# Two more attention pairs take the block-transposed load: pairs 6 and 7 of 32, one core

## The chip, the cores and the metric

The kernel runs on one core of a Trainium2 chip. The metric is device time in microseconds (us), the median over the runs shown. A core has a matrix engine (TensorE, PE in the profile; its weight loads are listed apart as PEld), VectorE (DVE), ScalarE (ACT), GpSimd (POOL) and SyncE (SP), which here issues nearly all DMAs. Each engine works through its own list of instructions in a fixed order and waits on semaphores for the others.

## The reference

The inputs are q, k and v of shape (8 batches, 8 heads, 576 tokens, 64), a feature matrix w_phi (64, 128), and float64 matrices of a token mixer (U, V) and of a channel MLP (w_ch1, w_ch2). Linear attention comes first, per batch and head:

```
def phi(x):
    proj = np.einsum('bhsd,df->bhsf', x, w_phi)
    proj = proj - np.max(np.abs(proj), axis=-1, keepdims=True)
    return np.concatenate([np.exp(proj), np.exp(-proj)], axis=-1)
q_p, k_p = (phi(q), phi(k))
kv = np.einsum('bhsf,bhsd->bhfd', k_p, v)
z = np.sum(k_p, axis=2)
num = np.einsum('bhsf,bhfd->bhsd', q_p, kv)
den = np.einsum('bhsf,bhf->bhs', q_p, z)[..., None] + 1e-06
return (num / den).astype(np.float32)
```

Then, with x of shape (8, 576, 512), u = x + (x^T U V)^T, and the output is u + relu(u w_ch1) w_ch2.

## The kernel before

**Pairs.** Attention is done for two heads of a batch at a time, a pair: four pairs in each of eight batches, 32 pairs, numbered here 0 to 31 as 4b + j. The 576 tokens of a head are 512 main tokens and a tail of 64. A `Pair` loads k and q (`raw`, two buffers, one for k and one for q), turns them so that the head dimension lies on the partitions (`transposes`), multiplies with w_phi (`project_k`, `project_q`), takes the maximum and the two exponentials (`k_features`, `q_features`), sums k features times v over the tokens (`kv_main`), and multiplies q features with the result (`out_main`).

**Two ways through a pair.** The flag `self.split` (L253) chooses. Without it (batches 0 and 1, pairs 0 to 7), k and q come in one DMA each of 256 KB (L270); TensorE turns them with eight 128x128 transposes (L322), ScalarE copies each result out of PSUM (L327), and the projections are plain float32 matmuls against the zero-padded `w_two` (L383 for k, L426 for q). A float32 matmul shows as two records in the trace. With it (batches 2 to 7, pairs 8 to 31), k and q come in eight DMAs of 32 KB each (L264), so that each 32x32 block lands where a transposition inside the blocks leaves the operand turned. VectorE turns the blocks in place (L314), ScalarE writes a rounded high part of each half (L317), VectorE the remainder (L318), and the projections are single-pass matmuls on these parts: L398 for k, whose two part sums are put together by a ScalarE copy (L401) and a VectorE addition (L402); L421 and L422 for q. The tail of 64 tokens is turned by TensorE in both ways (L304) and is split into parts by `stack` (L295, L296) only in the second. The order in which v is loaded (L286) and in which `out_main` writes follows the same flag.

**Buffers that order the pairs.** There is one `raw` buffer for k and one for q (L258). The loads of a pair start when the pair before has let go of them: in the first way after TensorE's transposes, in the second after the VectorE remainders at L318. `T0` and `T1`, the turned operands, have one buffer each; `T1` of a pair is free once the pair before it has made its second q projection.

**The weights and the MLP.** The float64 weights come in as words by DMA (L209, L212), sixteen blocks of two matrices. They are issued in the step of a pair behind that pair's last raw load (`issue_after(far.loaded.ins)`, with `LOADS`), and are converted block by block by ScalarE (L137, L138, L140, L234), VectorE (L141, L234, L235) and GpSimd (L145), spread over the steps 24 to 63 and ahead of their first use. The MLP of a batch (`hidden` L618, `add` L639, with `h_hi` L623 and `h_lo` L624) is cut into 32 chunks, which are mixed into the attention steps of later pairs. The MLP of batch 0 starts when batch 0 has its tokens mixed, some 92 us into the run, and runs beside pairs 5 to 9.

**What sets the order.** In the loop over pairs, step n projects k and q of pair n+1, makes the output of pair n, and loads and turns pair n+2 (`far`). The program is then ordered once, before it runs, by a scheduler that simulates the engines; on the chip each engine keeps to that order.

Of the kernel before, what the change touches and what calls it, by code (L numbers as in the profile page):

```python
# [25 lines left out]
def tile_kernel(  # L26
# [24 lines left out]
    NPAIR = H // 2  # L51
# [192 lines left out]


    SPLIT, Q = 2, 32

    class Pair:


        def __init__(self, b, j):
            self.b, self.h0, self.nm = b, 2 * j, f"{b}_{j}"
            self.split = b >= SPLIT  # L253
            self.tail = slice((b % 2) * ST, (b % 2 + 1) * ST)
            nm, hs = self.nm, slice(self.h0, self.h0 + 2)
            self.raw = []
            for n, src in enumerate((k, q)):
                m = raw.tile([P, 2, SM // 2], F32, tag="raw", bufs=2, name=f"raw{nm}_{n}")  # L258
                if self.split:
                    for i in range(4):  # L260
                        rs = slice(i // 2 * (SM // 2), (i // 2 + 1) * (SM // 2))
                        cs = slice(i % 2 * Q, (i % 2 + 1) * Q)
                        for g in range(2):
                            self.loaded = nc.sync.dma_start(  # L264
                                out=m[i * Q:(i + 1) * Q, g, :].rearrange(
                                    "c (j r) -> c j r", r=Q),
                                in_=src[b, self.h0 + g, rs, cs].rearrange(
                                    "(j c) r -> c j r", c=Q))
                else:
                    self.loaded = nc.sync.dma_start(  # L270
                        out=m, in_=src[b, hs, 0:SM, :].rearrange("h (p t) d -> p h (t d)", t=NT))
                self.raw.append(m)

            self.t_r = raw.tile([P, 2 * D], F32, tag="t_r", bufs=1, name=f"t_r{nm}")
            for n, src in enumerate((k, q)):
                nc.sync.dma_start(
                    out=self.t_r[n * ST:(n + 1) * ST, :].rearrange("r (h d) -> r h d", h=2),
                    in_=src[b, hs, SM:S, :].rearrange("h r d -> r h d"))
# [653 lines left out]
```

## The time and the profile before

| | |
|---|---|
| median of 3 runs | 1218.15 us (1218.03 to 1224.73) |
| the profiled execution | 1218.74 us, span 1216.9 us from first to last instruction |
| mean granted TensorE clock | 0.997 |
| busy: DVE, ACT, POOL | 668.7, 538.9, 204.5 us |
| DMA | 100.61 MB, mean 83 GB/s |

The span is the time from the first to the last instruction on the core; the profiled execution's own time is 1.84 us longer. The busy time of PE is that of matmul records, whose ends are modelled and which overlap, so that the mean duration of a record is longer than the time by which it holds back the next. The chain of work that ended last gives that second time, piece by piece. What belongs to one pair is told by the order of the records: of line 322 there are eight in each of pairs 0 to 7. The last two groups of eight, at 106.5 and 148.6 us, are those of pairs 6 and 7; line 314, which stands for pairs 8 to 31, starts at 157.1 us.

### The profile page before, as it was taken

The page shows a single profiled execution, that of the slowest core. Times are in us where ns is not written, and L with a number is a line of the kernel's source. Part 1 is how long each engine was busy: PE and PEld are TensorE (multiplying, and loading weights), DVE is VectorE, ACT ScalarE, POOL GpSimd, SP SyncE. Part 2 cuts the span into 40 slices and gives each one's busy share as a digit, 9 for nine tenths or more (in the row PEclk, how much of TensorE's full clock was granted, in tenths as well). Part 3 has the DMA queues.
Part 4 walks back from the last instruction along what each step waited for, and adds up shares of the span by engine and source line. Part 5 has one row for each costly group of instructions (what it writes and reads, how often), then busy time and mean ns, then how long its engine had stood idle before and what let it go on. Part 6 is the DMA issues. An engine that isn't in the chain of part 4 may idle for free.

```text
span 1216.9 us, 18254 instructions
## 1 busy us (share of the span) xinstructions
PE 1195.1 (98%) x6669; PEld 1031.3 (85%) x6669; DVE 668.7 (55%) x1482; ACT 538.9 (44%) x1151; POOL 204.5 (17%) x154
## 2 busy tenths in 40 slices
PE   8999998999999999999999999999999999999998
PEld 7878887888888888888888888888888888888886
DVE  5866777765556556755556656665656542311211
ACT  6867787454534445354435444344444431111110
POOL 3543443111111112011111111011101110000000
PEclk9999999999999999999999999999999999999999
DMA  4886021421245123431354123521343015410201
GB/s 132 262 279 210 29 50 28 134 64 30 65 108 116 30 52 79 109 81 25 72 125 104 28 59 88 120 46 33 99 92 99 1 53 149 115 35 1 69 1 35
DMA packets 248410, 100.61 MB, mean 83 GB/s; under 512 B 215424, under 2 KB 227968, under 8 KB 248320
## 3 DMA queue, kind: packets, MB, share of 16 engines
q1 hardware_dynamic: 248000, 98.92, 31.4%
q8 instruction: 53, 0.87, 0.3%
q10 hardware_dynamic: 320, 0.52, 0.1%
q14 instruction: 37, 0.30, 0.1%
HBM read 78.41 MB, written 20.97 MB: 82 GB/s over the span
## 4 chain that ended last, share of the span: by engine, by line
PE 80%; DVE 7%; SPq 5%; DMA 3%; ACT 3%; issue 2%; POOL 0%; DVEq 0%; ACTq 0%; POOLq 0%
PE ph L618 28%; PE o L639 28%; PE xp L481 7%; PE kv_ps L442 7%; SPq L604 3%; PE pp L560 2%; PE pk L398 1%; SPq L264 1%; PE kv_ps L435 1%; PE pq L421 1%; DMA u_dram<-x 1%; DMA y<-u_dram 1%; PE xpt L468 1%; PE pq L422 1%; DVE T L318 1%
## 5 line engine op out<-in xcount | busy, mean ns | idle before, releaser
L618 PE MATMUL ph<-uT_hi,w 128*128 128x512 f32 x1152 | 389.4, 395 | 1.2 <-ACT uT_hi L242 1.2
L639 PE MATMUL o<-w,h_hi 128*128 128x512 f32 x1152 | 329.4, 397 | 3.2 <-ACT h_hi L623 3.2
L618 PEld LDWEIGHTS ph<-uT_hi,w 128*128 128x128 f32 x1152 | 216.4, 188 | 46.9 <-ACT uT_hi L242 1.8
L639 PEld LDWEIGHTS o<-w,h_hi 128*128 128x128 f32 x1152 | 212.0, 189 | 45.6 <-ACT h_hi L623 4.9
L618 PE MATMUL ph<-uT_lo,w 128*128 128x512 f32 x576 | 225.1, 391 | 0.2 <-DVE uT_lo L243 0.2
L623 ACT ACTIVATE h_hi<-ph 128x512 fp32r<-128x512 f32 x144 | 86.0, 597 | 271.4 <-PE ph L618 260.4
L624 DVE SCALAR_TENSOR_TENSOR h_lo<-ph,h_hi 128x512 fp32r<-128x512 f32 x144 | 98.7, 686 | 176.9 <-ACT h_hi L623 175.7
L639 PE MATMUL o<-w,h_lo 128*128 128x512 f32 x576 | 192.1, 395 | 0.0
L362 POOL PARTITION_ALL_REDUCE qp<-qp x64 | 126.8, 1981 | 289.2 <-ACT qp L361 270.7
L481 PEld LDWEIGHTS xp<-kv,qp 128*128 128x128 f32 x1024 | 122.9, 192 | 4.8 <-ACT qp L365 1.3
L618 PEld LDWEIGHTS ph<-uT_lo,w 128*128 128x128 f32 x576 | 108.3, 188 | 21.5 <-DVE uT_lo L243 0.7
L442 PEld LDWEIGHTS kv_ps<-vb,kp 128*128 128x128 f32 x1024 | 124.0, 192 | 2.8
L442 PE MATMUL kv_ps<-vb,kp 128*128 128x65 f32 x1024 | 123.5, 270 | 0.0
L481 PE MATMUL xp<-kv,qp 128*128 128x65 f32 x1024 | 122.9, 272 | 0.6 <-ACT qp L365 0.6
L639 PEld LDWEIGHTS o<-w,h_lo 128*128 128x128 f32 x576 | 105.4, 188 | 20.2
L352 ACT ACTIVATE kp<-kp 128x512 f32<-128x512 f32 x64 | 40.4, 632 | 132.1 <-DVE kp L349 82.8
L362 POOL PARTITION_ALL_REDUCE qp_t<-qp_t x32 | 27.1, 846 | 399.8 <-ACT qp_t L361 399.8
L318 DVE TENSOR_TENSOR T<-raw,T 64x512 fp32r<-64x512 f32 x96 | 69.2, 720 | 33.4 <-ACT T L317 30.9
L314 DVE STREAM_TRANSPOSE raw<-raw 128x512 f32<-128x512 f32 x48 | 34.1, 711 | 83.3 <-DMA raw<-in_q_dram 34.3
L317 ACT CAST T<-raw 64x512 fp32r<-64x512 f32 x96 | 59.3, 618 | 33.5 <-PE pq L422 20.6
L364 ACT ACTIVATE qp<-qp 128x512 f32<-128x512 f32 x64 | 40.4, 632 | 55.4 <-DVE qp L363 54.8
L145 POOL INT64_ADD w_ab<-w_ab x32 | 44.7, 1398 | 69.3 <-DVE w_ab L141 68.5
(125 smaller groups left out, 1324.5 us busy)
## 6 DMA issues: line engine op xcount, KB each, us to landing
words<-in_moe_w_ch_dram SPq DMA_DIRECT2D x32, 512.0 KB, 9.0
w<-kept SPq DMA_DIRECT2D x30, 512.0 KB, 4.0
vb<-in_v_dram SPq DMA_DIRECT2D x64, 128.0 KB, 2.4
u_dram<-x SPq DMA_DIRECT2D x32, 256.0 KB, 2.2
st<-u_dram SPq DMA_DIRECT2D x16, 512.0 KB, 3.8
out_dram<-st SPq DMA_DIRECT2D x32, 256.0 KB, 2.4
y<-u_dram SPq DMA_DIRECT2D x112, 64.0 KB, 2.4
raw<-in_k_dram SPq DMA_DIRECT2D x192, 32.0 KB, 2.0
```

What stands on the lines that cost most here:

```text
L145: nc.gpsimd.int64_add(a64, a64, b64)
L317: nc.scalar.copy(out=m[here, s, :], in_=x_[here])
L318: nc.vector.tensor_sub(m[there, s, :], x_[here], f32(m[here, s, :]))
L352: nc.scalar.activation(out=kp[:, :, 0:F], in_=kp[:, :, F:2 * F], func=AF.Exp)
L362: nc.gpsimd.partition_all_reduce(qp[:, 0, :], qp[:, 1, :], P, ReduceOp.absmax)
L364: nc.scalar.activation(out=qp[:, 0, :], in_=qp[:, 1, :], func=AF.Exp)
L442: nc.tensor.matmul(self.kv_v[:, f, g, :], kp[:, t, f * F:(f + 1) * F], self.vb[:, g, t, :], start=False, stop=(t == NT - 1), skip_group_ch ...
L481: nc.tensor.matmul(xv[:, c, :], qp[:, f, c * P:(c + 1) * P], self.kv[:, f, c // 2 if self.split else s, :], start=(f == 0), stop=(f == 1))
L618: nc.tensor.matmul(ph, w1_part(f, l, c), r[:, c, :], start=(n == 0), stop=(n == 3 * NCC - 1))
L623: on_act = nc.scalar.activation(out=h_hi, in_=ph, func=AF.Relu)
L624: on_dve = nc.vector.scalar_tensor_tensor(out=h_lo, in0=ph, scalar=0.0, in1=f32(h_hi), op0=ALU.max, op1=ALU.subtract)
L639: ins = nc.tensor.matmul(self.o[t], l[:, cs], w2_t[f][:, r, :], start=(f == 0 and n == 0), stop=(f == NFC - 1 and n == 2))
```

## The change

The flag `split` of a pair no longer goes by the batch alone. It is set from pair 6 on, that is, for the third and fourth pair of batch 1 as well. Everything that asks the flag in `Pair` follows: the loads of k, q and v, the transposes, the split of the tail, the projections and the order of the output. The token mixer of batch 1 (`tokens`, which asks `tk.b >= SPLIT`) stays as it was.

```
     SPLIT, Q = 2, 32
+    BLOCKS_FROM = NPAIR + 2
...
             self.b, self.h0, self.nm = b, 2 * j, f"{b}_{j}"
-            self.split = b >= SPLIT
+            self.split = b * NPAIR + j >= BLOCKS_FROM
```

## The prediction

> **What bounds the kernel now.** I read the page first, then busy time by stretches of 10 us, then the waits of TensorE, then the chain of work and the engines' timelines around the two pairs.
>
> ```profile
> PE 1195.1 (98%) x6669; PEld 1031.3 (85%) x6669; DVE 668.7 (55%) x1482; ACT 538.9 (44%) x1151; POOL 204.5 (17%) x154
> ```
>
> TensorE is busy 98% of the span. The stretches tell where it is not (columns: from and to, length, then busy us of PE, PEld, DVE, ACT, POOL with instruction counts, granted clock, DMA share, GB/s).
>
> ```profile
> 80.00:90.00 10.00, 8.71 (x61) 7.56 (x62) 6.85 (x12) 8.12 (x15) 5.28 (x4) 1.00 0.93 295
> 90.00:100.00 10.00, 9.27 (x65) 8.15 (x64) 8.92 (x23) 6.41 (x12) 0.50 (x2) 1.00 0.91 302
> 100.00:110.00 10.00, 8.88 (x45) 7.30 (x44) 5.09 (x10) 6.54 (x15) 5.51 (x4) 1.00 0.14 33
> 110.00:120.00 10.00, 10.00 (x57) 8.72 (x56) 3.99 (x8) 9.34 (x19) 4.23 (x3) 1.00 0.94 318
> 190.00:200.00 10.00, 7.33 (x31) 6.13 (x31) 8.87 (x17) 7.42 (x16) 3.83 (x3) 0.83 0.22 39
> 200.00:1210.00 1010.00, 1007.14 (x5522) 868.59 (x5522) 528.96 (x1166) 387.69 (x843) 118.47 (x75) 1.00 0.28 69
> ```
>
> Up to 110 us TensorE has gaps, since the MLP of batch 0 has only begun and ScalarE and VectorE convert weights. From 110 us on it is full, but for one hole at 190 us, and from 200 us it misses only 2.9 us in 1010. So whatever is taken from TensorE's list after 110 us is gained, unless a new wait takes its place; and the only wait of size on TensorE in the stretch from 60 to 200 us is this:
>
> ```profile
> PE pkt L372 <- DVE tail_T L296: 3.1, 1, 3.1
> PE o L639 <- ACT h_hi L623: 1.1, 1, 1.1
> PE T L322 <- ACT tail_T L337: 0.9, 1, 0.9
> ```
>
> The 3.1 us stand at pair 8, the first pair that goes the second way, and thus are a sample of what the change makes twice more. How the hole came about, in order of time (start, length, engine, line; in brackets the idle time before it):
>
> ```profile
> 186.12 0.71 DVE L314 STREAM_TRANSPOSE raw<-raw 128x512 f32<-128x512 f32 x1 [3.73 <-issue]
> 187.77 0.28 DVE L296 TENSOR_TENSOR tail_T<-tT,tail_T 64x128 fp32r<-64x128 f32 x1
> 192.23 0.29 DVE L296 TENSOR_TENSOR tail_T<-tT,tail_T 64x128 fp32r<-64x128 f32 x1
> 192.67 0.30 PE L372 MATMUL pkt<-w_hl,tail_T 128*128 128x128 f32 x1 [3.11 <-DVE tail_T L296]
> 193.21 3.15 PE L639 MATMUL o<-w,h_hi 128*128 128x512 f32 x7
> ```
>
> VectorE stood 3.73 us before the block transposition of the next pair, whose k had not landed, and everything queued behind it was late, the tail of pair 8 among it. After the hole seven matmuls took 3.15 us, where twelve of line 639 elsewhere take 2.72 (below), 0.23 each, and the clock granted in the slice of 10 us fell to 0.83: (1 - 0.83) x 10 = 1.7 us. A hole of this kind costs 3.1 + 1.7 = 4.8 us.
>
> The Trainium skill, page "TensorE: Matmul & The Clock Gate", section "Part 1: The HAM clock gate", says that the clock is halved after at least one idle window of about 3.4 us and is given back after a busy one. Half the clock for 3.4 us is, as an estimate from that page, 1.7 us, which the 0.83 bears out; but by its threshold a hole of 3.11 us could pass without a drop, and here it did not. By the page's threshold such a hole would cost 3.1 us alone; the measurement decides, and I keep 4.8.
>
> **The change part by part.** *TensorE.* The chain of work gives what each piece holds the engine (start, length, what, count).
>
> ```profile
> 133.60 0.86 PE pk L383 x4
> 139.25 0.86 PE pq L426 x4
> 148.75 0.87 PE T L322 x8
> 196.78 0.24 PE pk L398 x2
> 202.65 0.29 PE pk L398 x2
> 210.84 0.29 PE pq L421
> 211.13 0.23 PE pq L422
> 214.23 2.72 PE o L639 x12
> ```
>
> Where the two pairs stand, from TensorE's timeline: the transposes of pair 6 and the first k projection of pair 6.
>
> ```profile
> 106.48 1.04 PE L322 MATMUL T<-ident,raw 128*128 128x128 f32 x8
> 124.85 1.03 PE L383 MATMUL pk<-w_two,T 128*128 128x256 f32 x4
> ```
>
> Per pair, before: eight transposes, 0.87; k projections, two of 0.86; q projections, two of 0.86; in all 0.87 + 1.72 + 1.72 = 4.31 us. After: the k projections are eight records, four pieces of 0.24 to 0.29, 0.96 to 1.16; the q projections two of 0.29 + 0.23, 1.04; in all 2.0 to 2.2. That saves 2.1 to 2.3 us a pair, and I take 2.2. The tail is projected by two records both before and after (lines 372 to 375, 410 to 413) and transposed once; I cost it at nothing. Both pairs: 4.4 us. All of it but pair 6's transposes at 106.5 us (0.87) lies after 110 us, where TensorE is the bound. The mean durations of the records would make the gain look twice as large; they overlap, so the spacing counts.
>
> *VectorE and ScalarE.*
>
> ```profile
> L314 DVE STREAM_TRANSPOSE raw<-raw 128x512 f32<-128x512 f32 x48 | 34.1, 711 | 83.3 <-DMA raw<-in_q_dram 34.3
> L318 DVE TENSOR_TENSOR T<-raw,T 64x512 fp32r<-64x512 f32 x96 | 69.2, 720 | 33.4 <-ACT T L317 30.9
> L317 ACT CAST T<-raw 64x512 fp32r<-64x512 f32 x96 | 59.3, 618 | 33.5 <-PE pq L422 20.6 <-DMA t_r<-in_k_dram 4.3 <-DMA w<-kept 2.5
> L327 ACT COPY T<-T 128x512 f32<-128x512 f32 x16 | 9.3, 585 | 3.6 <-PE pq L426 2.9 <-PE T L322 0.5
> L401 ACT COPY kp<-pk 128x256 f32<-128x256 f32 x96 | 33.3, 371 | 31.2 <-PE pk L398 31.0
> L402 DVE TENSOR_TENSOR kp<-pk,kp 128x256 f32<-128x256 f32 x96 | 37.5, 409 | 2.0 <-ACT kp L401 2.0
> L296 DVE TENSOR_TENSOR tail_T<-tT,tail_T 64x128 fp32r<-64x128 f32 x48 | 13.9, 290 | 27.6 <-ACT tail_T L295 27.1
> ```
>
> VectorE gains per pair two transpositions, four remainders, four additions and two tail remainders: 2 x 0.711 + 4 x 0.720 + 4 x 0.409 + 2 x 0.290 = 6.5 us, 13.0 for both. ScalarE gains four casts and four copies and loses two copies: 4 x 0.618 + 4 x 0.371 - 2 x 0.585 = 2.8 us, 5.6 for both. POOL loses one short memset a pair. The work falls between about 85 and 175 us. Taking the slices above as they stand, VectorE has 1 to 6 us free in every 10 and ScalarE 0.7 to 3.6 (the stretches from 80 to 120 us), so both fit without becoming the bound on average; TensorE hides them as long as the MLP of batch 0 supplies it. That cover is thin before 110 us: in the slice from 90 to 100 us VectorE is busy 8.92 of 10. If pair 6's two transpositions and its first two remainders land there ahead of what TensorE waits for, they cost up to 2 x 0.711 + 2 x 0.720 = 2.9 us. The other end is nothing, and a gain of up to 0.9 us is possible, since the wait of line 322 in that stage goes with the line. I take nothing, because the row nearest to it is the first projection that needs this work, pair 6's at 124.85 us, 15 us after that stage.
>
> *SyncE and the transfers.*
>
> ```profile
> 178.99 3.78 SPq L264 DMA_DIRECT2D raw<-in_k_dram  x8
> 107.40 0.55 SPq L270 DMA_DIRECT2D raw<-in_k_dram  x1
> raw<-in_k_dram SPq DMA_DIRECT2D x192, 32.0 KB, 2.0
> raw<-in_k_dram SPq DMA_DIRECT2D x8, 256.0 KB, 2.8
> L209 SPq DMA_DIRECT2D words<-in_moe_w_ch_dram x16: 432/461/949, 28.8 to 111.5; - x16
> L137 ACT ACTIVATE w_ab<-words x32: 762/783/822, 44.2 to 218.7; 128x512 uint16<-128x512 uint16 x32
> ```
>
> Eight block loads hold SP 3.78 us where one load held it 0.55, so a pair's k and q take 2 x (3.78 - 0.55) = 6.5 us more of the queue. An operand is there 3.78 + 2.0 = 5.8 us after its buffer is free, instead of 0.55 + 2.8 = 3.4. What is queued behind: the words of blocks 9 to 15, the v loads of the two pairs, and the stores of batch 0's tokens. Pair 7's q can also start only once pair 6's remainders are made, some ten us later than TensorE's transposes let it go before. So the last words, now issued by 111.5 us, go out perhaps 15 to 20 us later. Their conversions are 32 from 44.2 to 218.7 us, one every 5.6 us; block 13, the first of the last group, is number 26, about 190 us. The delay is hidden with tens of us to spare, and I cost it at nothing. If that cover went, the delay would go into the MLP of batch 0.
>
> *Waits moved.* Each of pairs 6 and 7 brings VectorE two transpositions that wait for DMA, with TensorE's operands (h_lo, line 624, the tail remainders and the maxima) queued behind. The price of one that goes wrong is 4.8 us, of one that is covered nothing. The first and the last of the six of pairs 8, 9 and 10, in the crowded stage:
>
> ```profile
> 157.14 0.70 DVE L314 STREAM_TRANSPOSE raw<-raw 128x512 f32<-128x512 f32 x1
> 233.67 0.71 DVE L314 STREAM_TRANSPOSE raw<-raw 128x512 f32<-128x512 f32 x1 [2.60 <-DMA raw<-in_q_dram]
> ```
>
> Of the six, one made a hole of that size; from 200 us on none did that counts. So I take none more and keep the hole at 190 us as it is; the ends are minus 4.8 (it goes) and plus 9.6 (two more).
>
> **The sum.** 1218.74 us (profiled; span 1216.9) - 4.4 + 0 + 0 = 1214.3 us. The profiled execution lies 0.6 us above the median of 1218.15, less than I can tell.
>
> **The rivals.** *One: the hole at 190 us goes as well.* Pair 8 would no longer be the first in block form, pair 7's q projection ends sooner and lets T1 go earlier, and the order is made anew. Against it: its cause, VectorE waiting for pair 9's k, is left as it was. It gives 1214.3 - 4.8 = 1209.5.
>
> *Two: the gain is eaten.* ScalarE's 9.34 of 10 between 110 and 120 us and VectorE's 8.92 between 90 and 100 speak for it: with 13.0 and 5.6 us more to do, these two pace the stage to 200 us and TensorE idles for what it saved. Against: TensorE stood full from 110 to 189 us beside them. It gives 1218.7, or 1217.2 if only the 2.9 us of the early slices are lost.
>
> *Three, on the other side: VectorE held at its queue's head.* Pair 7's k and pair 8's k now wait for the remainders of the pair before, each 5.8 us after release, as pair 9's did when the hole was made. One such hole gives 1214.3 + 4.8 = 1219.1, two give 1223.9; from one hole on the kernel is slower than before. For it: pair 8's hole, in the same crowded stage. Against: five transpositions of six passed, and tens of pairs later on.
>
> By the page's threshold named above, two such holes would leave the clock alone and give 1214.3 + 6.2 = 1220.5.
>
> **How the numbers follow.** The forecast, saving kept and hole unchanged, 1214.3, chance 40%; its own range is 1212 to 1217. Hole gone, 15%. Gain eaten, 22%. New holes, 23%: about 12 for one and 11 for two or more. The range from 1208.5 to 1222.5 leaves out two holes and more and a small part of the first rival, 15 to 20% in all. A measurement of this kernel can tell about 1%, 12 us, from no change: faster than 1206 needs more than the hole and the saving together, 4%; slower than 1230 needs three holes or more, 5%; the rest, 91%, is within.
>
> **What would show it.** Line 322 should have 48 records for 64, lines 383 and 426 also 48, and line 398 208 for 192. TensorE's busy time in the stretch from 110 to 200 us should do the same MLP work some 4 us sooner. Right: no new wait above 1 us on TensorE before 200 us. Wrong: a wait of TensorE on DVE or ACT of 3 us with a clock under 0.9 in the slice after it (rival three); TensorE below 9.5 of 10 between 110 and 180 us without one large wait (rival two); waits of L137 on the words' DMA (the cover that I gave the SP queue is not there).

## The result and the profile after

The changed kernel takes 1232.59 us (median of 7 runs, 1226.84 to 1234.86) against 1221.55 us for the kernel before (7 runs beside them, 1218.03 to 1224.73). The ratio is 1.0095, interval 1.0075 to 1.0116: 1% slower, where 1214.3 us was forecast. The ratios given here and below are not the quotients of the medians beside them, and differ from those by up to 0.0015. The profiled execution took 1234.85 us, 16.1 us more than that of before. Lines of the changed kernel from L246 on stand one higher than before.

The work that the change moves is there as forecast. The page's busy times and the counts by line (minimum, median and maximum duration in ns, first and last start in us):

```profile
PE 1205.8 (98%) x6645; PEld 1037.2 (84%) x6645; DVE 681.0 (55%) x1506; ACT 542.9 (44%) x1163; POOL 204.0 (17%) x152
```

```profile
L323 PE MATMUL T<-ident,raw x48: 272/273/421, 5.2 to 86.1; 128*128 128x128 f32 x48
L399 PE MATMUL pk<-w_hl,T x208: 274/282/384, 129.9 to 992.9; 128*128 128x256 f32 x104
```

TensorE has 24 records fewer, VectorE is 12.3 us busier than before and ScalarE 4.0. The difference in time lies early. The MLP makes `h_hi` 144 times in each kernel; its 21st and its 141st instance, in ScalarE's timeline (start, length), the kernel before first:

```profile
278.29 0.60 ACT L623 ACTIVATE h_hi<-ph 128x512 fp32r<-128x512 f32 x1
1190.00 0.60 ACT L623 ACTIVATE h_hi<-ph 128x512 fp32r<-128x512 f32 x1 [4.84 <-PE ph L618]
```

```profile
295.81 0.60 ACT L624 ACTIVATE h_hi<-ph 128x512 fp32r<-128x512 f32 x1
1205.97 0.60 ACT L624 ACTIVATE h_hi<-ph 128x512 fp32r<-128x512 f32 x1 [4.84 <-PE ph L619]
```

The changed kernel is 17.5 us behind at the 21st and 16.0 at the 141st. All of the loss is made before 300 us. Behind it the distance falls to 14.0 us by 388 us, is back at 16.1 after a wait of 1.8 us at 393 us, and then stays between 15.5 and 17.0.

**A part that is chance.** Up to 60 us TensorE does the same work in both. There it waits for `kp` in both, and what follows differs. TensorE's timeline, then the stretch from 60 to 70 us (the clock is the third number from the end), for before and for after:

```profile
59.57 0.71 PE L435 MATMUL kv_ps<-vt,kp_t 128*128 128x130 f32 x4 [1.65 <-DVE kp L349]
60.00:70.00 10.00, 10.00 (x79) 9.49 (x78) 6.19 (x16) 4.48 (x12) 4.31 (x4) 1.00 0.97 328
75.77 0.39 PE L560 MATMUL pp<-xs,u_all 128*128 128x256 f32 x1 [0.28 <-DMA vb<-in_v_dram]
```

```profile
59.44 0.71 PE L436 MATMUL kv_ps<-vt,kp_t 128*128 128x130 f32 x4 [1.68 <-DVE kp L350]
60.00:70.00 10.00, 10.00 (x48) 9.53 (x46) 2.55 (x7) 2.45 (x6) 2.63 (x2) 0.53 1.01 329
82.23 0.38 PE L561 MATMUL pp<-xs,u_all 128*128 128x256 f32 x1 [0.28 <-ACT xs L547]
```

A busy PE at 10.00 in both, 79 matmuls in one and 48 in the other: the clock fell to 0.53, and the same matmul starts 6.5 us later. The drop is not bound to the change: of the profiles below, those of the changed kernel with another loading and of pair 7 alone do not have it, and two variants of the kernel before do. Both profiles of the changed kernel itself have it, though, so chance is inferred here and not shown. The times fit: beside the first experiment, the kernel before took 1218.8 to 1222.4 us in 14 executions, with a mean clock of 0.996 to 0.999, and 1223.5 to 1227.6 in 15, with 0.990 to 0.996. The changed kernel's lower executions, 1228.2 to 1230.1, lie some 10 us above the lower ones of before. So of the 16.1 us between the two profiled executions I put 6.5 down to this, and some 10 to the change.

**Where the rest went.** Laying the starts of TensorE's matmuls in order, I charge each with its spacing in unbroken stretches (0.227 us for 512 columns, 0.12 for 256, 0.215 for a float32 record, about 0.1 for the small ones) and call the rest lost: waits, and time at a lower clock. In us, by stretch of the run, with the kernels of the next section beside the two:

| kernel | charged work | lost, all | 60-100 | 100-130 | 130-190 | 190-220 | 220-260 |
|---|---|---|---|---|---|---|---|
| before | 1167.4 | 42.7 | 6.4 | 2.0 | 4.5 | 1.9 | 1.9 |
| after | 1162.4 | 63.7 | 12.9 | 0.5 | 11.3 | 2.7 | 7.8 |
| after, whole loads | 1163.8 | 57.2 | 7.3 | 0.4 | 13.7 | 2.1 | 6.6 |
| pair 7 alone | 1165.2 | 52.7 | 6.4 | 1.8 | 7.8 | 1.9 | 4.9 |
| after, no remainders | 1163.5 | 53.8 | 13.5 | 2.5 | 4.0 | 0.5 | 6.2 |
| before, more turns | 1167.2 | 58.8 | 11.7 | 0.8 | 4.8 | 5.9 | 8.8 |
| before, more turns late | 1168.6 | 41.8 | 6.4 | 1.7 | 4.0 | 2.0 | 2.3 |
| from pair 9 | 1170.1 | 42.0 | 6.5 | 1.7 | 1.1 | 1.0 | 8.0 |

TensorE's list did become 5.0 us shorter. Against that stand 21.0 us more lost: 6.5 of chance between 60 and 100 us, 6.8 between 130 and 190, 5.9 between 220 and 260. The charge is good to some 1.5 us: the three kernels that begin with "after" have the same list, and are charged 1162.4 to 1163.8; so have before and the two with more turns, 1167.2 to 1168.6. TensorE's waits of 1 us and more in the changed kernel between 60 and 260 us, one instruction each:

```profile
PE xpt L469 <- DVE kp_t L350: 2.5, 1, 2.5
PE pq L422 <- DVE tail_T L297: 2.1, 1, 2.1
PE pkt L373 <- DVE tail_T L297: 1.5, 1, 1.5
PE pk L399 <- DVE uT_lo L243: 1.0, 1, 1.0
```

All four wait for VectorE. Those at 173.0, 159.9 and 253.4 us (the first, second and last) are new. The third, at 208.6 us, is the tail of pair 8, for which the kernel before waited 3.11 us at 192.67: the old hole has halved, and its clock drop is gone (1.00 between 200 and 220 us). Since the old hole's wait is in the 4.5 us of before between 130 and 190, the new holes there cost more than the difference of 6.8. The stretches (PE, PEld, DVE, ACT, POOL, clock, DMA share, GB/s) and the sum over the stage, after:

```profile
150.00:160.00 10.00, 7.93 (x57) 7.28 (x55) 5.52 (x15) 5.65 (x16) 1.94 (x1) 0.98 0.28 52
160.00:170.00 10.00, 10.00 (x36) 8.30 (x37) 6.81 (x10) 9.90 (x19) 5.48 (x4) 0.68 0.32 119
170.00:180.00 10.00, 7.50 (x31) 6.14 (x30) 8.97 (x22) 5.60 (x14) 4.24 (x3) 0.83 0.18 29
250.00:260.00 10.00, 7.81 (x35) 6.01 (x36) 7.34 (x20) 3.80 (x9) 0.00 (x0) 0.83 0.32 114
100.00:260.00 160.00, 149.96 (x806) 126.82 (x806) 122.93 (x250) 111.84 (x224) 55.93 (x37) 0.96 0.33 93
```

and before:

```profile
100.00:260.00 160.00, 155.11 (x881) 134.70 (x880) 113.11 (x232) 110.74 (x221) 59.27 (x41) 0.99 0.28 79
```

In the same 160 us TensorE gets through 75 matmuls fewer (in part because its list is 24 records shorter and runs later), and VectorE is busy 122.9 us for 113.1, still with 37 us free. So VectorE is not full on average; it is late at single places. This is the place at 170 us: VectorE's timeline, with the matmuls that wait for it and two of the GpSimd instructions beside it. The matmuls of line 640 are the first six of eight.

```profile
164.74 0.42 DVE L141 TENSOR_SCALAR w_ab<-w_ab 128x512 int32<-128x512 int32 x1
165.86 1.07 DVE L141 TENSOR_SCALAR w_ab<-w_ab 128x512 int32<-128x512 int32 x1 [0.25 <-ACT w_ab L140]
166.84 0.68 DVE L235 TENSOR_TENSOR w<-w_ab,w 128x512 fp32r<-128x512 f32 x1
167.55 1.67 DVE L319 TENSOR_TENSOR T<-raw,T 64x512 fp32r<-64x512 f32 x1
169.26 1.28 DVE L234 CAST w<-w_ab 128x512 fp32r<-128x512 f32 x1
170.57 0.69 DVE L319 TENSOR_TENSOR T<-raw,T 64x512 fp32r<-64x512 f32 x1
...
172.55 0.28 DVE L350 TENSOR_TENSOR kp_t<-pkt,mk_t 128x128 f32<-128x128 f32 x1
167.09 1.58 POOL L145 INT64_ADD w_ab<-w_ab  x1 [0.45 <-PE ph L619]
168.66 2.55 POOL L363 PARTITION_ALL_REDUCE qp<-qp  x1
169.45 0.28 PE L374 MATMUL pkt<-w_hl,tail_T 128*128 128x128 f32 x1
172.98 1.01 PE L469 MATMUL xpt<-kv,qp_t 128*128 128x130 f32 x4 [2.50 <-DVE kp_t L350]
173.64 2.91 PE L640 MATMUL o<-w,h_hi 128*128 128x512 f32 x6
```

TensorE had projected pair 7's tail by about 169.7 us; the 0.28 us subtraction that turns it into `kp_t` started 2.8 us later, behind weight conversions (L234, L235) and split remainders (L319) without a gap between them. The two remainders, the seventh and eighth of their line, are pair 7's for q: work that the change added. TensorE stood 2.50 us, and then six matmuls of line 640 took 2.91 us, 0.49 each, for 0.23 at full clock.

The matmul that stood, `xpt`, does not read `kp_t`. By the kernel, attention has three PSUM tiles (`BANKS`), into which TensorE writes. Here `pkt` and two of `pk` held them, and `xpt` started 0.15 us after the subtraction, the last to read `pkt`, was done. In the same way `pq` at 159.9 us waited for the tile that the tail's remainder reads, and `pk` at 253.4 for that of u^T. Only `pkt` at 208.6 us waited for something that it reads itself. So VectorE holds TensorE up less by operands than by tiles that it is late to empty. This is read from the kernel and the rows; no run had more tiles.

The hole at 159.9 us begins with a transfer. The k of pair 8 can be loaded only when pair 7's remainders have let go of the buffer, at 149.64 us, and is issued from 149.66 us on. VectorE stands at its transposition, ScalarE then waits for what VectorE has queued behind it, and the tail's second remainder waits for ScalarE:

```profile
156.61 0.71 DVE L315 STREAM_TRANSPOSE raw<-raw 128x512 f32<-128x512 f32 x1 [1.97 <-DMA raw<-in_k_dram]
158.52 0.63 ACT L365 ACTIVATE qp<-qp 128x512 f32<-128x512 f32 x1 [3.88 <-DVE qp L364]
159.47 0.29 DVE L297 TENSOR_TENSOR tail_T<-tT,tail_T 64x128 fp32r<-64x128 f32 x1 [0.67 <-ACT tail_T L296]
159.91 0.77 PE L422 MATMUL pq<-T,w_hl 128*128 128x512 f32 x1 [2.07 <-DVE tail_T L297]
```

With the clock at 0.68 in the slice behind it, (1 - 0.68) x 10 = 3.2 us, this hole costs 2.1 + 3.2 = 5.3 us, and the one at 173 us, with 0.83, costs 2.5 + 1.7 = 4.2. Both are estimates from these rows.

At 250 us the hole is another one: the MLP of batch 0 is done and the operands of batch 1's are still being made. TensorE's timeline, after, then the same place before:

```profile
251.88 0.49 PE L619 MATMUL ph<-uT_hi,w 128*128 128x512 f32 x1 [0.68 <-ACT uT_hi L242]
253.40 0.47 PE L399 MATMUL pk<-w_hl,T 128*128 128x256 f32 x2 [1.03 <-DVE uT_lo L243]
254.84 0.59 PE L619 MATMUL ph<-uT_lo,w 128*128 128x512 f32 x1 [0.48 <-DVE uT_lo L243]
...
259.06 1.89 PE L482 MATMUL xp<-kv,qp 128*128 128x65 f32 x16
```

```profile
239.77 1.90 PE L481 MATMUL xp<-kv,qp 128*128 128x65 f32 x16
...
242.78 0.51 PE L618 MATMUL ph<-uT_hi,w 128*128 128x512 f32 x1 [0.44 <-ACT uT_hi L242]
243.51 0.50 PE L618 MATMUL ph<-uT_lo,w 128*128 128x512 f32 x1 [0.22 <-DVE uT_lo L243]
```

Before, sixteen output matmuls of attention bridge the gap, and the waits for u^T's two parts are 0.44 and 0.22 us. After, the same sixteen stand behind the gap, at 259 us, and the waits are 0.68, 1.03 and 0.48 us, with the clock at 0.83. VectorE's timeline, after, shows what came ahead of u^T's low part:

```profile
249.21 2.47 DVE L661 TENSOR_TENSOR st<-st,o 128x512 f32<-128x512 f32 x4
...
252.57 0.68 DVE L243 TENSOR_TENSOR uT_lo<-pt,uT_hi 128x512 fp32r<-128x512 f32 x1
```

The four additions finish the MLP of batch 0. Before, the same four came behind this instruction: it started at 236.54 us, they at 238.32.

### The profile page after: what moved, and what is told of

Same layout as the page of the kernel before. It is cut to its first block, busy times and chain, and to the rows that moved or that the text cites. A ratio compares the mean times of both kernels' runs of the same rounds, so it can differ in the third digit from the quotient of the medians.

```text
span 1233.1 us, 18269 instructions
## 1 busy us (share of the span) xinstructions
PE 1205.8 (98%) x6645; PEld 1037.2 (84%) x6645; DVE 681.0 (55%) x1506; ACT 542.9 (44%) x1163; POOL 204.0 (17%) x152
## 4 chain that ended last, share of the span: by engine, by line
PE 80%; DVE 6%; SPq 4%; DMA 4%; ACT 4%; issue 1%; POOL 0%; ACTq 0%; DVEq 0%; POOLq 0%
PE ph L619 28%; PE o L640 27%; PE xp L482 8%; PE kv_ps L443 7%; SPq L605 3%; PE pk L399 2%; PE pp L561 1%; PE kv_ps L436 1%; PE pq L422 1%; DMA y<-u_dram 1%; DMA u_dram<-x 1%; PE xpt L469 1%; PE pq L423 1%; SPq L265 1%; DVE T L319 1%
## 5 line engine op out<-in xcount | busy, mean ns | idle before, releaser
L443 PEld LDWEIGHTS kv_ps<-vb,kp 128*128 128x128 f32 x1024 | 127.5, 196 | 3.1
L443 PE MATMUL kv_ps<-vb,kp 128*128 128x65 f32 x1024 | 126.8, 275 | 0.0
L319 DVE TENSOR_TENSOR T<-raw,T 64x512 fp32r<-64x512 f32 x104 | 76.2, 733 | 34.8 <-ACT T L318 32.1
L318 ACT CAST T<-raw 64x512 fp32r<-64x512 f32 x104 | 64.3, 618 | 31.6 <-PE pq L423 21.9
L315 DVE STREAM_TRANSPOSE raw<-raw 128x512 f32<-128x512 f32 x52 | 37.0, 711 | 69.8 <-DMA raw<-in_k_dram 35.6
```

What stands on the lines that cost most here:

```text
L318: nc.scalar.copy(out=m[here, s, :], in_=x_[here])
L319: nc.vector.tensor_sub(m[there, s, :], x_[here], f32(m[here, s, :]))
L443: nc.tensor.matmul(self.kv_v[:, f, g, :], kp[:, t, f * F:(f + 1) * F], self.vb[:, g, t, :], start=False, stop=(t == NT - 1), skip_group_ch ...
```

## The experiments

The theory formed from these rows: the 13 us of added VectorE work, in the stage that converts the weights, make VectorE late for TensorE. The rivals: the block loads and their transfers; the new order of the lists by itself; chance. All kernels except those that say otherwise start from the changed kernel or from the one before, with the threshold as a number in place of `NPAIR + 2` on the line of `SPLIT`, which leaves the line numbers of the kernel before. Each ratio is to the kernel before on the same chip.

**The changed kernel again.**

```
-    SPLIT, Q = 2, 32
+    SPLIT, Q, BLOCKS_FROM = 2, 32, 6
...
-            self.split = b >= SPLIT
+            self.split = b * NPAIR + j >= BLOCKS_FROM
```

> The changed kernel once more, the new constant put on an existing line, so that its line numbers are those of the kernel before. It is there for the clock: in the profiled execution of the changed kernel TensorE ran at half clock from 60 to 75 us, after a wait of 1.68 us that the kernel before has as well (1.65 us) and among the same instructions; that alone set it back by 6.5 us. If that drop is chance, the executions of this kernel fall in two groups some 6 us apart, and the profiled one may have no drop at 60 us; the median stays 9 to 12 us above the kernel before. If the change brings it about, every execution has it and the profile shows a clock near 0.53 from 60 to 70 us again.

Measured: 1232.36 us (1228.16 to 1234.44, 12 runs) for 1223.51 (29 runs), ratio 1.0058, interval 1.0038 to 1.0078. The loss is real; its largest wait is the one shown above, `xpt` for `kp_t`, here 4.3 us. The hole at 159.9 us is not there: VectorE stands only 0.49 us for the k of pair 8. The profile has the drop after 60 us again, at 0.66. The executions fall in two groups, five from 1228.2 to 1230.1 us and seven from 1232.2 to 1234.4, but these lie 3 us apart and not 6, so how often this kernel has the drop stays open.

**One pair instead of two.**

```
-    SPLIT, Q, BLOCKS_FROM = 2, 32, 6
+    SPLIT, Q, BLOCKS_FROM = 2, 32, 7
```

> Only pair 7 goes over to blocks; pair 6 keeps TensorE's transposes. Crowding theory (VectorE and ScalarE, busy with the weights from 100 to 220 us, fall behind by the work added, and TensorE waits for PSUM banks that they are late to empty): half the added work, so about half the loss, 4 to 7 us over the kernel before. Chance theory (the loss is clock drops that any order may meet, and a reordered program): no order by the number of pairs; anything from -2 to +12. Transfer theory (16 DMAs a pair on the SP queue hold up the words): pair 6's loads stand right before eight words' DMAs, pair 7's before six; half the loss.

Measured: 1226.48 us, ratio 1.003 (1.001 to 1.005). Its profile has the full clock all through, and yet a span of 1224.7 us, 7.8 more than before's: 2.2 us less work, 10.0 more lost. So no drop of the clock is needed for the loss, and one pair makes part of it. The transfer theory foretold half the loss as well, so this run does not part the two.

**One pair fewer than before.**

```
-    SPLIT, Q, BLOCKS_FROM = 2, 32, 6
+    SPLIT, Q, BLOCKS_FROM = 2, 32, 9
```

> The other direction: pair 8 also keeps TensorE's transposes, blocks from pair 9 on. Crowding theory: 6.5 us of VectorE and 2.8 us of ScalarE work leave the crowded stage, the hole of 3.1 us and its clock drop at 190 us go; TensorE gets 2.2 us more work: 0 to 3 us faster than the kernel before. Theory of the prediction (TensorE's work alone counts): 2.2 us slower. Chance theory: between -3 and +8.

Measured: 1222.06 us, ratio 1.0 (0.9978 to 1.0021). Pair 8 the first way costs TensorE 2.7 us of work. The theory expected up to 3 us gained, and nothing is. The hole at 190 us is gone (TensorE is busy 10.00 of 10 there, at the full clock), but one at 235 us, at the start of batch 1's MLP, takes its place:

```profile
230.00:240.00 10.00, 7.18 (x29) 5.52 (x28) 5.07 (x10) 2.56 (x6) 0.00 (x0) 0.83 0.23 77
...
PE pk L398 <- DVE uT_lo L243: 2.4, 1, 2.4
```

**The remainders on GpSimd.** The remainders of pairs 6 and 7, four to a pair, go to the engine that is least busy.

```
+                    b_late = self.b >= SPLIT
...
-                        nc.vector.tensor_sub(m[there, s, :], x_[here], f32(m[here, s, :]))
+                        (nc.vector if b_late else nc.gpsimd).tensor_sub(m[there, s, :], x_[here], f32(m[here, s, :]))
```

> As the changed kernel, but for pairs 6 and 7 the four remainders of k and q are subtracted by GpSimd instead of VectorE: 2 x 4 x 0.72 = 5.8 us leave VectorE in the crowded stage; nothing else changes, loads and TensorE's work are the same. Crowding of VectorE: the waits of TensorE on the tail's remainder and on kp_t shrink, 3 to 7 us faster than the changed kernel. If GpSimd's subtraction is several times slower than 0.72 us, the raw buffers are held longer and the gain is gone. Chance or transfer theory: no systematic change against the changed kernel.

Measured: 1281.66 us, ratio 1.046 (1.0427 to 1.0492). As a test of the theory it failed, for a reason of its own. GpSimd's timeline (in brackets its idle time before):

```profile
140.92 1.27 POOL L319 TENSOR_TENSOR T<-raw,T 64x512 fp32r<-64x512 f32 x1 [6.99 <-issue]
148.08 1.25 POOL L145 INT64_ADD w_ab<-w_ab  x1 [5.89 <-issue]
...
164.05 1.95 POOL L363 PARTITION_ALL_REDUCE qp<-qp  x1 [6.57 <-issue]
```

The subtraction itself takes 1.25 to 1.3 us, but each change between it and the other two kinds of instruction leaves GpSimd idle for some 6 to 7 us, and everything that waits for it is late.

**The remainders left out.** For pairs 6 and 7, ScalarE casts all 128 partitions and VectorE makes no remainder. The kernel thus leaves out the low parts of k and q of these pairs, and adds in their place the values of other tokens, so their results are not the reference's. Loads, turns, casts and projections stay.

```
+                        if self.b < SPLIT:
+                            here = slice(0, P)
                         nc.scalar.copy(out=m[here, s, :], in_=x_[here])
-                        nc.vector.tensor_sub(m[there, s, :], x_[here], f32(m[here, s, :]))
+                        if self.b >= SPLIT:
+                            nc.vector.tensor_sub(m[there, s, :], x_[here], f32(m[here, s, :]))
```

> As the changed kernel, but the four remainders of k and q of pairs 6 and 7 are left out (ScalarE's cast writes all 128 partitions instead of 64, at the same length), so the low parts of these pairs are not in the result. TensorE's list, the loads, ScalarE's instructions and VectorE's transpositions stay. That takes 2 x 4 x 0.72 = 5.8 us of the 13.0 us that the change gave VectorE, and frees the raw buffers earlier. Crowding theory: TensorE's waits between 130 and 190 us shrink, 1225 to 1229 us (the changed kernel 1232, the kernel before 1223). Transfer theory, or a loss that is only a matter of the order: 1230 to 1234.

Measured: 1221.82 us (1218.46 to 1230.61), ratio 1.0004 (0.9983 to 1.0025), below the 1225 to 1229 us expected. Without eight VectorE instructions of 0.72 us, 5.8 us in all, the kernel takes as long as the kernel before. In the table, the lost time falls by 9.9 us, from 63.7 to 53.8, and from 130 to 190 us it is 4.0 us for 11.3; this profile has the drop at 60 us too. What is still lost between 220 and 260 us, 6.2 for 1.9, uses up TensorE's shorter list, so the saving of 4.4 us does not appear even here. The waits for `kp_t` and the tails are gone; its largest, at 60 us, is the 1.6 us for `kp`, which the profile of before has as well.

The edit does more than free VectorE: `raw` is let go without waiting for remainders, and VectorE stands 0.58 us for pair 8's k instead of 1.97. How much belongs to VectorE's time and how much to this, the run does not tell. The changed kernel run again had the short stop, 0.49 us, and kept the loss, so the stop alone is not the cause.

**Whole loads.** The changed kernel, but k and q of pairs 6 and 7 come in one DMA each, so that SP's queue has their loads as before; their blocks then lie in other places, and their results are not the reference's.

```
-                if self.split:
+                if self.split and b >= SPLIT:
```

> As the changed kernel, but k and q of pairs 6 and 7 come in one DMA each of 256 KB, as before the change, instead of eight of 32 KB. The blocks then lie in the wrong places, so these pairs' results are not the reference's; all work of the engines stays. Transfer theory (6.5 us more of the SP queue a pair, words, v and stores behind it, VectorE waiting for blocks): 1224 to 1228 us. Crowding theory: the DMA waits of VectorE at line 314 before 160 us go (2 to 3 us in all), the rest stays: 1229 to 1233.

Measured: 1230.96 us (4 runs), ratio 1.0087 (1.0071 to 1.0104). Nothing is given back: the eight block loads of pairs 6 and 7, and what they take of SP's queue, are not the cause. Pair 8's k still comes in eight, and VectorE still stands 1.75 us ahead of its transposition, at 151.0 us. The largest wait on VectorE is still there, longer than in the changed kernel's first profile:

```profile
PE xpt L468 <- DVE kp_t L349: 3.9, 1, 3.9
```

This profile, like that of before, has no drop at 60 us, and is the clean comparison: span 1227.5 for 1216.9 us, which is 3.6 us less work and 14.5 us more lost, to within 0.3. Of the 14.5, 9.2 lie between 130 and 190 us and 4.7 between 220 and 260.

**More MLP work in hand.** Six chunks of the MLP are held back at the points where a mixer needs cover, instead of four; once in the changed kernel, once in the kernel before.

```
-    HELD = 4
+    HELD = 6
```

> As the changed kernel, but six of the MLP's chunks of a batch are held back for the change of batches instead of four (HELD). Of the time that the changed kernel loses against the kernel before, the spacing of TensorE's matmuls puts 4 to 6 us between 220 and 260 us, where the MLP of batch 0 runs out while VectorE still makes batch 1's tokens. If TensorE lacks work there, two chunks more, 2 x 12 x 0.227 = 5.4 us, cover it: 1227 to 1230. If it waits there for buffers that VectorE is late with, whatever the chunks: 1231 to 1234.

> The kernel before with HELD at six, as the control of the run above. The kernel before loses only 1.9 us to spacing between 220 and 260 us, so by either theory it stays within 3 us of 1223; if it gets slower or faster by more than that, HELD acts on all batches and the run above is to be read against this one.

Measured: changed 1224.44 us, ratio 1.0033 (1.0015 to 1.005); before 1219.91, ratio 1.0008 (0.999 to 1.0026). Against the ratios of 1.0058 and 1.0095 measured for the changed kernel, and 1.0087 with whole loads beside this run, 3 to 8 us come back, with the same VectorE work; none come back in the kernel before. The profile of this variant of the kernel before also has the drop after 60 us, in its worst slice 0.66, with 56 matmuls for 79.

**VectorE work alone, early and late.** The kernel before, with raw k and q of pairs 6 and 7 turned four times in place (which undoes itself), 11.4 us of VectorE work; and the same work in pairs 18 and 19.

```
                 else:
+                    if self.b == 1 and self.h0 >= 4:
+                        x_ = self.raw[n].rearrange("p h e -> p (h e)")
+                        for _ in range(4):
+                            nc.vector.transpose(out=x_, in_=x_)
```

```
-                    nc.vector.transpose(out=x_, in_=x_)
+                    for _ in range(5 if self.b == 4 and self.h0 >= 4 else 1):
+                        nc.vector.transpose(out=x_, in_=x_)
```

> The kernel before, with VectorE work alone added: in pairs 6 and 7 (which stay in the first way) VectorE turns the blocks of raw k and raw q four times in place, which leaves them as they were, before TensorE transposes them. That is 16 transpositions of 0.711 us, 11.4 us of VectorE work in the stage from 100 to 200 us, with four waits of VectorE for a transfer, and nothing saved on TensorE. Crowding of VectorE (my theory now): the time rises by most of what the changed kernel lost, 6 to 12 us over the kernel before, with TensorE waits on kp_t, tail_T or h_hi made by VectorE. If the loss came from the PSUM tiles and casts of the split way rather than from VectorE's time, the kernel stays within 3 us of the kernel before.

> The same VectorE work as in the run with turns only, at another place: pairs 18 and 19 of batch 4 turn raw k and raw q five times in place instead of once, 16 more transpositions of 0.711 us, 11.4 us of VectorE work, some 400 us later, where VectorE is busy about half the time and converts no weights. Crowding (my theory): what counts is how much VectorE has free in that stage, so the time stays within 2 us of the kernel before. If any VectorE work put ahead of TensorE's operands, or any new order of the list, costs what it did in the early stage: 6 us over the kernel before.

Measured: early 1229.9 us (12 runs), ratio 1.0065 (1.004 to 1.0089); late 1222.65 us (12 runs), ratio 1.002 (1.0 to 1.0039), with a profiled span of 1217.2 us, 0.3 above before's. The same VectorE work costs 6.4 us by the medians in one place and 2.1 in the other, and TensorE's list is not touched in either. The turns also hold back k and q and wait for transfers, so they are not VectorE time alone. The place of the loss differs from the changed kernel's, though: by the table the early turns lose nothing more between 130 and 190 us, and 10.9 us more between 190 and 260. So added VectorE work in this stage has a price, but the holes at 159.9 and 173 us are those of the split way.

**The conversions spread over more steps.**

```
-    CONVERT = (24, 63)
+    CONVERT = (24, 70)
```

> The changed kernel, with the weight conversions spread over the steps 24 to 70 instead of 24 to 63, so that VectorE and ScalarE have less to convert in the stage in which pairs 6 and 7 run. Crowding of VectorE: part of the loss is given back, 3 to 8 us less than the changed kernel (1224 to 1229), unless the later conversions make blocks of the second MLP late. If the order of the two ways, and not the amount of work, makes the holes: within 2 us of the changed kernel.

> Control for the run before it: the kernel before with the conversions spread over the steps 24 to 70. It has 13 us less VectorE work in that stage and only one hole to lose, so by the crowding theory it gains little, 0 to 3 us against the kernel before; if it gains as much as the changed kernel does, the spread is worth something by itself and says nothing of the change.

Measured: changed 1236.73 us, ratio 1.0112 (1.0088 to 1.0136); before 1231.6 us, ratio 1.0073 (1.005 to 1.0097). Both expectations missed, and in both kernels for a reason near to the exception that the first named: weights come too late. The same wait of TensorE on a converted weight stands in each:

```profile
PE o L639 <- DVE w L234: 4.7, 1, 4.7
```

The conversions have no room to be later. The distance between the two kernels stays, 5.1 us, so this pair neither supports nor refutes the theory.

No version was faster than the kernel before: from pair 9 on, without remainders, and with six chunks held in the kernel before, the ratios' intervals include 1.

## Why the prediction was wrong

**TensorE's 4.4 us: right.** The charged work fell by 5.0 us, by 3.6 with whole loads, by 2.2 for one pair, and rose by 2.7 where pair 8 went back, each good to some 1.5. The counts of records are those foretold.

**SyncE and the words: right.** The last words go out at 137.0 us for 111.5, some 25 us later rather than 15 to 20, and line 137 never waits for words. Restoring the loads gave nothing back.

```profile
L209 SPq DMA_DIRECT2D words<-in_moe_w_ch_dram x16: 432/466/739, 28.8 to 137.0; - x16
L137 ACT ACTIVATE w_ab<-words x32: 764/779/802, 44.0 to 232.3; 128x512 uint16<-128x512 uint16 x32
```

**VectorE's 13.0 us: right in size, wrong in price.** This is the step that failed: "both fit without becoming the bound on average; TensorE hides them". Busy time rose by 12.3 us, and 37 us of VectorE's 160 stayed free, as forecast. But the engine works in a fixed order, and the free time lay elsewhere. What stood ahead of `kp_t` was a run of conversions and remainders without a gap. In the clean comparison 14.5 us more were lost, not 0, and 9.2 of them in the stretch where this shows; taking out 5.8 us of VectorE's work, with what that does to the buffers, gave back some 10.

The profile of before had the warning, and I gave it only half its cause. Of the hole at 190 us I wrote that VectorE was late because a transfer held it at 186 us. VectorE's timeline of the kernel before goes on from there:

```profile
188.09 1.10 DVE L234 CAST w<-w_ab 128x512 fp32r<-128x512 f32 x1
189.22 2.26 DVE L318 TENSOR_TENSOR T<-raw,T 64x512 fp32r<-64x512 f32 x2
191.51 0.69 DVE L235 TENSOR_TENSOR w<-w_ab,w 128x512 fp32r<-128x512 f32 x1
```

These 4.1 us of remainders and conversions, back to back, stood between the stop and the tail remainder at 192.23 that TensorE waited for.

**"I take none more" holes, and the old one "as it is": wrong.** Two new holes came before 200 us, and the old one shrank from 3.1 us to 1.5, without its clock drop. The price of 4.8 us for a hole was right in size: the two cost 5.3 and 4.2. The mark for rival three was a wait of 3 us and a clock under 0.9: the waits of the profiled execution were 2.5 and 2.1 us, but 4.3 when the kernel ran again and 3.9 with whole loads, with the clock at 0.78 and 0.84 in the slice after. Its mechanism, VectorE held by the k of pair 8, made the hole at 159.9 us. The hole at 173 us comes nearer to rival two: VectorE busy with conversions and added work. But "TensorE idles for what it saved" capped that rival's loss at the saving, and nothing in the kernel sets such a cap. That VectorE also empties the PSUM tiles which TensorE needs next was in none of the rivals.

With these terms, all from the profiled executions, the forecast becomes 1214.3 + 5.3 + 4.2 for the new holes, less 3.3 for what the old one lost, 5.9 between 220 and 260 us and 6.5 for the drop at 60 us: 1232.9 us, for 1234.85 in the profiled execution.

**What stays open.** Some 5 to 6 us of the loss lie between 220 and 260 us, where TensorE waits for the operands of batch 1's MLP. It shows in nearly every kernel whose list was ordered anew early, also in that from pair 9 on, which has less VectorE work than before (8.0 us for 1.9). So the new order probably makes part of it. In the changed kernel one step of it is the four additions that moved ahead of u^T's low part; in the kernel from pair 9 on it is another, since there VectorE stands 2.50 us for a DMA ahead of 234.76 us. No run put the additions back. Nor was VectorE's time ever parted from the buffers that its work holds, in `raw` and in PSUM. Holding more chunks gave back 3 to 8 us of time in total, but in its one profile not at this place (7.6 us).

## What to carry to other kernels

Free time of an engine on average is no cover for work added ahead of another engine's operand; read the queue of the engine that is to take the work, instruction by instruction, in front of each small operand that the bound engine waits for and of each tile that it needs emptied. When a rival says that a gain is eaten, do not end its price at the gain. And an order that fits at one seam between phases can lose at that seam what is gained ahead of it, so look there before counting a saving.

## What the runs showed of the hardware

TensorE's clock fell after single waits of 1.68 to 2.5 us, in some executions and not in others of the same instructions: at 59.5 us after a wait of 1.68 us in the profile of after, and not after 1.65 in that of before. It costs about 6.5 us there. The Trainium skill, page "TensorE: Matmul & The Clock Gate", section "Part 1: The HAM clock gate", gives about 3.4 us of idleness, in a window that runs freely, as what halves the clock; no single wait there is that long in the rows, so the threshold is not borne out here as a limit for one wait. That the phase of the window decides would fit, but no run tested it.

GpSimd stood idle 5.9 to 7.0 us at the three changes shown in the rows above between a plain subtraction and its other instructions. That run has ten such changes: nine of them took 5.9 to 7.3 us, and the first 10.0, with a wait for words in it. The Trainium skill, page "GPSIMD Engine Reference", section "2.1 Instruction dispatch", names about 6 us for the first call of freshly loaded code. The size agrees; the runs show it at every change back and forth.

Some VectorE instructions beside a GpSimd instruction took longer. By the rows at 165 to 170 us, line 319 took 1.67 us for a mean of 0.72 (of line 318, the same before the change), line 234 1.28 and line 141 1.07 where the same instruction at 164.74 took 0.42 (beside the 1.07 us, GpSimd's line 145 ran from 165.36 for 1.28 us). Not all do: at 170.57 line 319 took 0.69 beside the 2.55 us instruction.

The Trainium skill, page "SBUF — State Buffer", section "SBUF: two separate sides", says that the two engines share a port which one of them holds for a whole instruction. The three agree with that, the one at 170.57 does not show it, and the three lengthen the run of work ahead of `kp_t` by some 2 us. That this made the hole was not tried.
